# A fused attention and mixture-of-experts kernel: fewer float32 key tiles, a narrowing step through PSUM, two more early weight rooms, a new order of all steps

## The chip, the cores and the metric

The kernel runs on one core of one Trainium2 chip, in a single launch. The metric is the device time of that launch in microseconds (us). PE is the matrix engine, DVE the vector engine, ACT the scalar engine, POOL GpSimd; SP and ACT also issue DMAs. SBUF is the on-chip memory of 128 partitions, PSUM the accumulators that PE writes.

## The reference

Three stages follow each other. All inputs are float32, but `w_in` and `w_out` reach the kernel as float64.

```python
# attention: batch 2, heads 8, sequence 768, head size 64, 16 clusters
q_assign = np.argmax(np.einsum('bhsd,hcd->bhsc', q_n, c_n), axis=-1)   # k_assign alike
mask = q_assign[:, :, :, None] == k_assign[:, :, None, :]
scores = np.where(mask, scale * np.matmul(q, k.transpose(0, 1, 3, 2)), -1000000000.0)
scores = scores - np.max(scores, axis=-1, keepdims=True)
attn = np.exp(scores); attn = attn / (np.sum(attn, axis=-1, keepdims=True) + 1e-09)
x = np.matmul(attn, v)                       # then 1536 tokens x 512
# feed-forward with a gate, hidden size 2048
h = x @ w_in
g = h * np.clip(h + 3.0, 0.0, 6.0) / 6.0
x = (g @ w_out).astype(np.float32)
# soft mixture of 8 experts, 4 slots each, hidden size 1024
logits = x @ phi
d = softmax(logits, axis=0); slot_input = d.T @ x
slot_out[e] = np.maximum(slot_input[e] @ w1[e], 0.0) @ w2[e]
c = softmax(logits, axis=1); return c @ slot_out
```

(`softmax` stands here for the maximum, exponential and division that the reference writes out.)

## The kernel before

**Tiles.** The 16 pairs of batch and head are 16 heads, i = 0 to 15, each with 768 queries and 6 key tiles of 128 (t = 0 to 5). The 1536 tokens are 12 tiles of 128, called tokens 0 to 11 here; tokens 0 to 5 need heads 0 to 7, tokens 6 to 11 need heads 8 to 15. Values that need more than 16 bits are kept as a pair of float16 parts: `high` (an ACT copy to float16, L333) and `low` (POOL subtracts the high part, L343).

**A head.** PE computes masked scores for the row maxima (`sm`, L507), DVE reduces them (`mxs`, L523), PE computes scores again with the maxima folded in (`st`, L545 and L549), ACT takes the exponential, and `pv` multiplies the probabilities by the values. A key tile that `WHOLE` lists for its head goes through `pv` as float32: ACT writes `pp` once (L586) and PE does 6 float32 products (L615; the trace shows each as 2 matmuls, 12 for a tile). Any other key tile goes as a float16 pair: ACT writes `p` (L593) and its high part (L333), POOL the low part (L343), and PE does 6 + 6 + 6 float16 matmuls (L620, L621, L628). Score tiles stand in the PSUM pool `ps_s`, which has three rooms; `sm`, `st`, the transposes `gp` and others take turns in them.

**Weights of the feed-forward.** Half of each float64 word is handled at a time. `narrow` turns 1024 float64 a partition into float32: ACT takes the absolute value of the high word with a scale (L850), DVE shifts it left by 3 (L852), DVE joins the sign bit (L855), DVE joins the low word's top bits (L860). There are 16 of these, 8 of `wi` and 8 of `wod`, all in the time of heads 0 to 7. `wphi3` splits the product of `w_out` and `phi` into a high and a low part (L943, L945, L946).

**A token.** `hid` multiplies 128 tokens by the input weights (`h`, L684; a token is 48 matmuls of 512 columns), `act` forms the gate as a float16 pair `ghl`, and the pair is turned over, either by DMA transposes on SP's queue (L712) or, for tokens in `TURNED`, by PE (L721, to PSUM tiles `gp`) with two copies by ACT (L727) and two by DVE (L725). `gt` is one buffer for all tokens. `logits` (L736, L737) reads it.

**The tail.** Slot inputs (`zt`, `si`, `sit`), layer 1 of the experts (`e`, L1289), layer 2 (`o`, L1326 and, in column parts, L1346), then the slots' outputs are spread over the tokens (`so` L1241, `po` L1266) and written (L1279). Expert weights come in chunks of 1 MB named `wk_n`, two DMAs each on SP's queue (`fetch`, L1007; the last four in column parts, L988). Each chunk needs a room: `rooms` lists them in order. The first 4 are in ring a, 11 in ring b, 7 in buffers that the earlier stages free; the chunks after that wait until the first are used. `selectors` (L1230) is 24 small POOL copies that build a 0/1 matrix for `so`.

**What sets the order.** Every piece of work is a generator that is cut into steps at each `yield`; it is registered with `ev`, and the numbers in the string `ORDER` say from which generator the next step is taken. `ROOMS` fixes which buffer of its pool each tile takes. So the program order on each engine is written out, and each engine takes its instructions in that order; waits are by semaphores. A DMA queue's instruction waits for its buffer to be free, and what stands behind it on the same queue waits too.

## Time and profile before

| | us |
|---|---|
| three timed runs | 501.71, 502.46, 504.79 (median 502.46) |
| the profiled execution | 500.38 |
| its span in the trace | 498.2 |
| busy: PE, DVE | 447.5, 288.9 |
| busy: ACT, POOL | 314.1, 238.1 |

The span runs from the first instruction to the last; the profiled execution is 2.2 us longer than its span. Busy times are unions of the instructions' times on an engine; matmuls overlap each other there, so a busy PE is not PE at its peak. The page of the profile counts 93.4 MB by DMA.

### The profile page before, as it was taken

Reading aid. Unit: us, or ns where it says so; the run is one execution under the profiler, and the core shown is the slowest. Engines: PE = TensorE matmul, PEld = TensorE weight load, DVE = VectorE, ACT = ScalarE, POOL = GpSimd, SP = SyncE. Lnnn points to the kernel's source line nnn. Section 1 sums busy time; section 2 is a strip of 40 time slices with the busy share of each in tenths; the row PEclk is TensorE's granted clock in tenths of the full one; section 3 lists DMA queues with packets and bytes.
Section 4 is the critical chain, followed back from the end, with each engine's and each line's share of the span. In section 5 each row is a group of like instructions: output and inputs, shape, how many; then the busy total and the mean of one; then the engine's idle time right before and its main releaser. Section 6 shows DMA issues by size and latency. Waiting matters only on the chain.

```text
span 498.2 us, 11989 instructions
## 1 busy us (share of the span) xinstructions
PE 447.5 (90%) x5014; PEld 291.7 (59%) x5014; DVE 288.9 (58%) x489; ACT 314.1 (63%) x499; POOL 238.1 (48%) x217
## 2 busy tenths in 40 slices
PE   2699899998999989999999999979999999789773
PEld 1467787786876457556665766744555554623252
DVE  3889999898869665745728678412433254411322
ACT  4687888898865548778796977953445455501021
POOL 3435746856544336677686795973132236000000
PEclk9999999999999979999999999999999999889998
DMA  5799888659772985457559361018999305899996
GB/s 189 199 212 217 224 196 234 154 164 239 240 226 52 236 147 78 93 124 144 107 114 257 71 118 34 2 22 136 278 403 410 147 1 156 294 372 382 335 287 204
DMA packets 125622, 93.41 MB, mean 187 GB/s; under 512 B 88193, under 2 KB 111233, under 8 KB 125569
## 3 DMA queue, kind: packets, MB, share of 16 engines
q1 hardware_dynamic: 120832, 86.85, 65.7%
q10 hardware_dynamic: 4736, 5.80, 3.5%
q8 instruction: 39, 0.64, 0.5%
q14 instruction: 15, 0.11, 0.1%
HBM read 64.06 MB, written 7.34 MB: 143 GB/s over the span
## 4 chain that ended last, share of the span: by engine, by line
PE 53%; DVE 18%; DMA 8%; ACT 6%; POOL 6%; issue 6%; SPq 2%; DVEq 0%; POOLq 0%; ACTq 0%
PE h L684 15%; DVE mxs L523 5%; PE sm L507 5%; PE acc L615 5%; PE st L545 4%; PE st L549 4%; POOL ghl L343 3%; DMA wk<-in_moe_w_dram 3%; PE e L1289 2%; DMA wod<-in_moe_w_out_dram 2%; SPq L1007 2%; PE acc L628 2%; PE acc L620 2%; PE acc L621 2%; POOL pp L343 2%
## 5 line engine op out<-in xcount | busy, mean ns | idle before, releaser
L343 POOL TENSOR_TENSOR pp<-p,pp 128x768 f16<-128x768 f32 x62 | 105.4, 1707 | 71.0 <-ACT pp L333 26.4
L684 PE MATMUL h<-wq,xt 128*128 128x512 f16 x576 | 132.6, 379 | 0.6 <-DMA xt<-xhl 0.6
L523 DVE TENSOR_REDUCE mxs<-sm 128x1 f32<-128x768 f32 x96 | 88.7, 953 | 23.5 <-PE sm L507 22.9
L684 PEld LDWEIGHTS <-xt 128*128 128x128 f16 x576 | 55.2, 98 | 61.1 <-issue 1.3
L343 POOL TENSOR_TENSOR ghl<-r,ghl 128x1024 f16<-128x1024 f32 (+1 forms) x25 | 50.2, 2011 | 66.0 <-ACT ghl L333 65.9
L593 ACT ACTIVATE p<-st 128x768 f32<-128x768 f32 x62 | 49.9, 807 | 15.7 <-PE st L549 13.3
L333 ACT ACTIVATE pp<-p 128x768 f16<-128x768 f32 x62 | 52.0, 842 | 1.7 <-PE acc L628 0.5
L545 PE MATMUL st<-qk1t 128*128 128x384 f16 x192 | 48.7, 336 | 2.6 <-DVE qk2t L532 1.1
L615 PE MATMUL acc<-v,pp 128*128 128x65 f32 x408 | 50.1, 274 | 0.0
L615 PEld LDWEIGHTS acc<-v,pp 128*128 128x128 f32 x408 | 48.6, 192 | 1.7 <-ACT pp L586 0.3
L703 DVE SCALAR_TENSOR_TENSOR r<-r,h 128x1024 f32<-128x1024 f32 (+1 forms) x26 | 29.5, 1135 | 34.2 <-ACT r L701 34.2
L549 PE MATMUL st<-qk2t 102*128 102x384 f16 x192 | 48.6, 335 | 0.4 <-DVE qk2t L532 0.4
L507 PE MATMUL sm<-qk2t 80*128 80x384 f16 x192 | 45.6, 341 | 3.5 <-DVE qk2t L387 1.7
L343 POOL TENSOR_TENSOR qk<-qk,qk 128x768 f16<-128x768 f32 x15 | 26.8, 1787 | 30.3 <-ACT qk L333 29.7
L701 ACT ACTIVATE r<-h,b_relu 128x1024 f32<-128x1024 f32 (+1 forms) x26 | 27.2, 1047 | 19.0 <-POOL ghl L343 13.8
L333 ACT ACTIVATE ghl<-r 128x1024 f16<-128x1024 f32 (+1 forms) x26 | 25.7, 988 | 21.4 <-DVE r L703 19.7
L620 PE MATMUL acc<-v,pp 128*128 128x65 f16 x372 | 31.4, 193 | 2.0 <-DVE mv L494 1.9
L621 PE MATMUL acc<-v,pp 128*128 128x64 f16 x372 | 31.4, 194 | 0.0
L586 ACT ACTIVATE pp<-st 128x768 f32<-128x768 f32 x34 | 26.6, 808 | 6.9 <-PE st L549 6.7
L620 PEld LDWEIGHTS <-pp 128*128 128x128 f16 x372 | 27.0, 99 | 2.7 <-issue 0.3
L621 PEld LDWEIGHTS <-pp 128*128 128x128 f16 x372 | 25.4, 97 | 4.5 <-issue 2.4
L549 PEld LDWEIGHTS <-qk2t 102*128 102x128 f16 x192 | 19.2, 100 | 14.4 <-issue 2.5
(190 smaller groups left out, 792.3 us busy)
## 6 DMA issues: line engine op xcount, KB each, us to landing
wk<-in_moe_w_dram SPq DMA_DIRECT2D x60, 512.0 KB, 9.0
wi<-in_moe_w_in_dram SPq DMA_DIRECT2D x16, 512.0 KB, 5.6
wod<-in_moe_w_out_dram SPq DMA_DIRECT2D x16, 512.0 KB, 4.8
wos<-wo ACTq DMA_DIRECT2D x8, 512.0 KB, 4.5
wk<-wos SPq DMA_DIRECT2D x8, 512.0 KB, 5.9
qk<-in_q_dram SPq DMA_DIRECT2D x16, 192.0 KB, 3.3
qk<-in_k_dram SPq DMA_DIRECT2D x16, 192.0 KB, 3.7
v<-in_v_dram SPq DMA_DIRECT2D x16, 192.0 KB, 3.6
```

The costliest lines, as they stand in the source:

```text
L333: nc.scalar.activation(out, in_, AF.Copy, scale=scale)
L343: (nc.vector if e == "v" else nc.gpsimd).tensor_tensor(out=out, in0=in_, in1=hi, op=ALU.subtract)
L507: nc.tensor.matmul(s[:, j, 0:384], d["qk2t"][0:80, n, 0], d["qk2t"][0:80, 3 * j : 3 * j + 3, 1], start=True, stop=True,)
L523: nc.vector.tensor_reduce(out=mxs[i % 2][:, 96 + n : 97 + n], in_=s[:, :, 0:384], op=ALU.max, axis=AX.XY)
L545: nc.tensor.matmul(s[:, j, 0:384], d["qk1t"][:, t, 1], d["qk1t"][:, 3 * j : 3 * j + 3, 0], start=True, stop=False)
L549: nc.tensor.matmul(s[:, j, 0:384], d["qk2t"][0 : 96 + NT, t, 1], d["qk2t"][0 : 96 + NT, 3 * j : 3 * j + 3, 0], start=False, stop=True,)
L593: nc.scalar.activation(p32, s[:, :, 0:384], AF.Exp, scale=sc_exp)
L615: nc.tensor.matmul(o, p32[:, j, r * P : (r + 1) * P], d["v32"][:, t], start=(t == 0 and n == 0), stop=False)
L620: nc.tensor.matmul(o, hi, v1[:, t, 0:65], start=(t == 0 and n == 0), stop=False)
L621: nc.tensor.matmul(o[:, 0:64], hi, v1[:, t, 65:129], start=False, stop=False)
L684: nc.tensor.matmul(s[:, fb % 2], xt[:, lhs], wq[fb][:, hl, kk], start=(n == 0), stop=(n == 11))
L703: nc.vector.scalar_tensor_tensor(out=g, in0=r, scalar=6.0 * SG, in1=sf, op0=ALU.min, op1=ALU.mult)
```

## The change

1. `WHOLE` names three key tiles for each of heads 0 to 7 ("024") in place of 3 to 5: 24 float32 key tiles rather than 34.
2. `narrow`: DVE takes the sign bit first, from the high word into SBUF; ACT writes the absolute value to a PSUM tile `nt` of the pool `ps_s`; one DVE step shifts it and joins the sign, in place; the last DVE step joins the low word as before.
3. `wphi3`: ACT writes the high part from PSUM, one DVE step makes the low part from PSUM. The float32 copy `wpf` and one DVE copy are gone.
4. The first square root is called by a dummy (`warm_0`) right at the start of `centroids`, before the centroids are there.
5. `TURNED` loses tokens 8 and 9: their gates are turned by DMA.
6. `rooms` has two more entries: chunk 15 lies half in a buffer of the tokens' input tiles `xt` (now 3 buffers of two tokens) and half in the pool of the selector matrix; chunk 20 lies half in `xt` and half in a buffer of `r`. 24 chunks rather than 22 have a room before the first is used. Small tiles of the tail (`c16`, `cT`, `sel`, `s16`, `h1`, `hts`, `o2s`, `zts`, `sis`) lie in freed weight rooms.
7. `ORDER` and `ROOMS` are new from beginning to end; `selectors` stands after the slot inputs.

```diff
-    "2 2 2 1 3 9 3 9 10 10 2 2 10 10 10 10 10 11 280 1 8 6 11 12 32 12 325 96 178 280 292 84 84 137 137 80 80 284 36 "
+    "1 1 3 0 1 1 2 8 2 795 8 9 9 9 9 9 4 1 5 5 9 9 10 0 0 9 5 13 13 5 796 796 6 6 56 10 11 56 57 11 797 798 12 801 "
...
-WHOLE = ("01245", "01245", "01245", "0124", "024", "0124", "0124", "0124", "", "", "", "", "", "", "", "")
-TURNED = {6, 7, 8, 9, 10, 11}
+WHOLE = ("024", "024", "024", "024", "024", "024", "024", "024", "", "", "", "", "", "", "", "")
+TURNED = {6, 7, 10, 11}
...
     def centroids():
         c32 = ap.tile([P, D], F32, tag="acp", name="c32", bufs=1)
         nc.scalar.dma_start(out=c32, in_=cent.rearrange("h c d -> (h c) d"))
+        nc.gpsimd.memset(b_relu, 3.0 * SG)
+        nc.scalar.activation(sm.tile([P, 1], F32, tag="nm", name="warm_0", bufs=4), b_relu, AF.Sqrt)
...
         if part == 0:
-            t = ap.tile([P, 1024], U32, tag="nw", name=f"nw_{nm}", bufs=1)
-            raw[nm, "t"] = t
+            t = raw[nm, "t"] = pss(f"nt_{nm}").rearrange("p a b -> p (a b)").bitcast(U32)
+            s = raw[nm, "s"] = ap.tile([P, 1024], U32, tag="nw", name=f"nw_{nm}", bufs=1)
+            nc.vector.tensor_scalar(out=s, in0=hi, scalar1=0x80000000, scalar2=None, op0=ALU.bitwise_and)
+            yield
             nc.scalar.activation(t.bitcast(F32), hi.bitcast(F32), AF.Abs, scale=2.0**-111)
-            yield
-            nc.vector.tensor_scalar(out=t, in0=t, scalar1=3, scalar2=None, op0=ALU.logical_shift_left)
         elif part == 1:
             t = raw[nm, "t"]
             nc.vector.scalar_tensor_tensor(
-                out=t, in0=hi, scalar=0x80000000, in1=t, op0=ALU.bitwise_and, op1=ALU.bitwise_or
+                out=t, in0=t, scalar=3, in1=raw.pop((nm, "s")), op0=ALU.logical_shift_left, op1=ALU.bitwise_or
             )
...
-        wf = sm.tile([P, 4, NS], F32, tag="l4", name=f"wpf_{j}", bufs=1)
-        nc.scalar.activation(wf, po, AF.Copy, scale=SPH / SW)
-        yield
-        nc.vector.tensor_copy(wp2[:, 4 * j : 4 * j + 4, 0:NS], wf)
-        nc.vector.tensor_tensor(
-            out=wp2[:, 4 * j : 4 * j + 4, NS : 2 * NS], in0=wf, in1=wp2[:, 4 * j : 4 * j + 4, 0:NS], op=ALU.subtract
+        wh = wp2[:, 4 * j : 4 * j + 4, 0:NS]
+        nc.scalar.activation(wh, po, AF.Copy, scale=SPH / SW)
+        yield
+        nc.vector.scalar_tensor_tensor(
+            out=wp2[:, 4 * j : 4 * j + 4, NS : 2 * NS], in0=po, scalar=SPH / SW, in1=wh, op0=ALU.mult, op1=ALU.subtract
         )
...
-    rooms = ["a"] * NRA + ["b"] * NRB + ["w0", "w1", "w2", "w3", "ghl", "gt", "ghl"]
+    rooms = ["a"] * NRA + ["b"] * NRB + ["x.g", "w0", "w1", "w2", "w3", "x.r", "ghl", "gt", "ghl"]
+    rooms += ["a"] * 2 + ["b"] * 10
```

Three places show how the order moves work. The first is DVE at the start of head 0, before: `qk1t` and `qk2t` are the turned queries and keys, `as` and `mx` the cluster scores and their maxima, `nw_i0_0` and `wi_0_0` the first piece that is narrowed, `mxs` the row maxima.

```order
L387 COPY qk1t_0_152<-tq1_153 128x6x128
L436 TENSOR_REDUCE mx_0_212<-as_0_168 128x12
L437 TENSOR_TENSOR as_0_168<-as_0_168,mx_0_212 128x192
L445 TENSOR_TENSOR as_0_168<-as_0_168,rank_87 128x192
L448 TENSOR_REDUCE mx2_0_216<-as_0_168 128x12
L450 TENSOR_TENSOR oh_0_218<-as_0_168,mx2_0_216 128x6x2x16
L852 TENSOR_SCALAR nw_i0_0_247<-nw_i0_0_247 128x1024
L855 SCALAR_TENSOR_TENSOR nw_i0_0_247<-wi_0_0_222,nw_i0_0_247 128x1024
L860 SCALAR_TENSOR_TENSOR wi_0_0_222<-wi_0_0_222,nw_i0_0_247 128x1024
L387 COPY qk2t_0_257<-tq2_258 128x6x128
L523 TENSOR_REDUCE mxs_0_110<-sm_0_0_282 128x1
```

The same place after:

```order
L383 COPY qk1t_0_159<-tq1_160 128x6x128
L850 TENSOR_SCALAR nw_i0_0_240<-wi_0_0_153 128x1024
L432 TENSOR_REDUCE mx_0_248<-as_0_182 128x12
L433 TENSOR_TENSOR as_0_182<-as_0_182,mx_0_248 128x192
L441 TENSOR_TENSOR as_0_182<-as_0_182,rank_87 128x192
L444 TENSOR_REDUCE mx2_0_254<-as_0_182 128x12
L446 TENSOR_TENSOR oh_0_256<-as_0_182,mx2_0_254 128x6x2x16
L855 SCALAR_TENSOR_TENSOR nt_i0_0_239<-nt_i0_0_239,nw_i0_0_240 128x1024
L860 SCALAR_TENSOR_TENSOR wi_0_0_153<-wi_0_0_153,nt_i0_0_239 128x1024
L383 COPY qk2t_0_265<-tq2_266 128x6x128
L850 TENSOR_SCALAR nw_i0_1_314<-wi_0_1_262 128x1024
L519 TENSOR_REDUCE mxs_0_110<-sm_0_3_310 128x1
```

The sign step (L850) of a piece now stands ahead of the cluster maxima and does not need ACT; two steps rather than three stand between the one-hot matrix `oh` and the copy of `qk2t`, and the next piece's sign step stands ahead of the first row maximum.

The second place is SP's queue in the time of tokens 6 to 9, before: `xt_8` is the input of token 8, `wk_3` and the others are chunks of expert weights (`wos` is a product of `w_out` that the kernel wrote to memory itself).

```order
L669 DMA_TRANSPOSE xt_8_5502<-xhl_1_2904 128x8x128
L1007 DMA wk_3_5551<-wos_100 128x2x512 x2
L1007 DMA wk_4_5554<-in_moe2_w1_dram 128x1024
L1007 DMA wk_2_5470<-wos_100 128x2x512
L1007 DMA wk_4_5554<-in_moe2_w1_dram 128x1024
L1007 DMA wk_1_5468<-wos_100 128x2x512
L1007 DMA wk_5_6373<-in_moe2_w1_dram 128x1024
L1007 DMA wk_6_6375<-in_moe2_w1_dram 128x1024
```

After, `gt_8` and `gt_9` are the turned gates of tokens 8 and 9:

```order
L1011 DMA wk_12_6048<-in_moe2_w1_dram 128x1024
L1011 DMA wk_13_6050<-in_moe2_w1_dram 128x1024
L710 DMA_TRANSPOSE gt_8_6065<-ghl_8_5904 128x16x128 x2
L1011 DMA wk_4_5861<-in_moe2_w1_dram 128x1024
L1011 DMA wk_14_6105<-in_moe2_w1_dram 128x1024
L1011 DMA wk_1_5847<-wos_100 128x2x512
L1011 DMA wk_13_6050<-in_moe2_w1_dram 128x1024
L1011 DMA wk_0_4731<-wos_100 128x2x512
L1011 DMA wk_3_5852<-wos_100 128x2x512
L710 DMA_TRANSPOSE gt_9_6140<-ghl_9_6029 128x16x128
L1011 DMA wk_2_5849<-wos_100 128x2x512
L710 DMA_TRANSPOSE gt_9_6140<-ghl_9_6029 128x16x128
```

Four DMA transposes of gates now stand among the weight loads, where before only loads followed the last input transpose.

The third place is the end of SP's queue. Before, `wk_32` to `wk_35` are the last four chunks in column parts and `ob` the output tiles:

```order
L988 DMA wk_32_6721<-in_moe2_w2_dram 128x4x128
L988 DMA wk_33_6722<-in_moe2_w2_dram 128x4x128
L988 DMA wk_34_6723<-in_moe2_w2_dram 128x4x128
L1279 DMA out_0_dram<-ob_0_3_6912 128x2x256
L988 DMA wk_35_6724<-in_moe2_w2_dram 128x4x128
L1279 DMA out_0_dram<-ob_0_1_6901 128x2x256
```

After:

```order
L989 DMA wk_32_6959<-in_moe2_w2_dram 128x4x128
L989 DMA wk_33_6960<-in_moe2_w2_dram 128x4x128
L1296 DMA out_0_dram<-ob_0_3_6983 128x2x256
L989 DMA wk_34_6961<-in_moe2_w2_dram 128x4x128
L989 DMA wk_35_6962<-in_moe2_w2_dram 128x4x128
L1296 DMA out_0_dram<-ob_0_1_6993 128x2x256
```

Two weight loads rather than one stand behind the first output DMA.

## Rows read from the trace of the kernel before

**Rows 1.** Windows by stage: start and end, length, busy us of PE, PEld, DVE, ACT, POOL, PE clock.

```profile
25.00:331.00 306.00, 294.24 (x3534) 210.25 (x3533) 221.69 (x362) 240.76 (x366) 194.20 (x128) 0.99 0.65 150
...
336.00:425.00 89.00, 84.27 (x722) 45.60 (x722) 30.91 (x51) 43.72 (x75) 30.17 (x39) 1.00 0.69 221
425.00:450.00 25.00, 19.74 (x223) 10.09 (x224) 7.29 (x20) 5.07 (x16) 0.16 (x1) 0.86 0.91 336
```

**Rows 2.** Waits of PE: line, what it waited for, us in total, times, longest.

```profile
PE o L1346 <- DMA wk<-in_moe_w_dram: 3.3, 3, 2.4
```

**Rows 3.** Chain of waits, first 32 us: start, length, what.

```profile
3.53 1.28 ACT L815
4.82 0.21 ACT cy L815
```

**Rows 4.** Timeline of PE around a float32 and a float16 key tile: start, length, what.

```profile
36.53 1.45 PE L615 MATMUL acc<-v,pp 128*128 128x65 f32 x12
37.81 0.19 PE L620 MATMUL acc<-v,pp 128*128 128x65 f16 x1
...
38.18 1.25 PE L507 MATMUL sm<-qk2t 80*128 80x384 f16 x6
39.28 0.35 PE L628 MATMUL acc<-v,pp 128*128 128x65 f16 x6
39.46 1.75 PE L615 MATMUL acc<-v,pp 128*128 128x65 f32 x14
```

**Rows 5.** The page's groups: the float16 pairs' copies by POOL and ACT.

```profile
L343 POOL TENSOR_TENSOR pp<-p,pp 128x768 f16<-128x768 f32 x62 | 105.4, 1707 | 71.0 <-ACT pp L333 26.4
...
L333 ACT ACTIVATE pp<-p 128x768 f16<-128x768 f32 x62 | 52.0, 842 | 1.7 <-PE acc L628 0.5
```

**Rows 6.** Instructions by line: minimum, median, maximum in ns, first and last start.

```profile
L850 ACT ACTIVATE nw_i<-wi x8: 1131/1135/1143, 11.2 to 115.9; 128x1024 f32<-128x1024 f32 x8
L852 DVE TENSOR_SCALAR nw_o<-nw_o x8: 683/690/695, 86.4 to 185.6; 128x1024 uint32<-128x1024 uint32 x8
L855 DVE SCALAR_TENSOR_TENSOR nw_i<-wi,nw_i x8: 1224/1226/2295, 15.0 to 120.7; 128x1024 uint32<-128x1024 uint32 x8
L860 DVE SCALAR_TENSOR_TENSOR wo<-wod,nw_o x8: 1217/1226/2645, 96.7 to 188.3; 128x1024 uint32<-128x1024 uint32 x8
L945 DVE CAST wp<-wpf x4: 219/772/1672, 143.2 to 206.4; 128x128 f16<-128x128 f32 x4
L946 DVE TENSOR_TENSOR wp<-wpf,wp x4: 293/590/1629, 143.4 to 207.7; 128x128 f16<-128x128 f32 x4
L703 DVE SCALAR_TENSOR_TENSOR r<-r,h x26: 686/1213/1223, 176.9 to 424.5; 128x1024 f32<-128x1024 f32 x22, 128x512 f32<-128x512 f32 x4
```

**Rows 7.** Timeline of POOL and DVE at one narrowing step.

```profile
112.75 1.65 POOL L343 TENSOR_TENSOR pp<-p,pp 128x768 f16<-128x768 f32 x1 [2.25 <-ACT pp L333]
112.84 2.65 DVE L860 SCALAR_TENSOR_TENSOR wo<-wod,nw_o 128x1024 uint32<-128x1024 uint32 x1
```

**Rows 8.** Chain of waits, 380 to 414 us.

```profile
397.84 0.89 PE gp L721 x16
398.73 5.18 PE h L684 x24
```

**Rows 9.** Landing of the 12 gate transposes that SP issues at L712.

```profile
DMA to landing us min/median/max: 4.2/4.9/7.6
```

**Rows 10.** DMA in 336 to 430 us: GB/s in 40 slices of 2.35 us.

```profile
GB/s 64 167 47 211 192 169 321 241 209 363 288 405 409 413 415 408 411 406 413 410 404 415 394 105 0 3 0 7 0 0 0 0 0 94 199 258 211 352 396 77
```

**Rows 11.** Chain of waits, 425 us to the end.

```profile
465.07 8.90 DMA wk<-in_moe_w_dram
...
480.02 4.76 DMA out_dram<-ob
...
484.79 4.05 DMA wk<-in_moe_w_dram
```

**Rows 12.** Timeline of POOL around the selectors.

```profile
415.81 3.66 POOL L1230 COPY sel<-ident 32x4 f32<-32x4 f32 x24
```

More of the change, by code (lines that the diff above doesn't have):

```diff
@@ L289, in clustered_attention_ffn_softmoe @@
     mvs = [ap.tile([P, 129], F16, name=f"mv_{i}", bufs=1) for i in range(3)]
-    def first():
-        nc.gpsimd.memset(b_relu, 3.0 * SG)
-        yield
-        nc.scalar.activation(sm.tile([P, 1], F32, tag="nm", name="warm_0", bufs=4), b_relu, AF.Sqrt)
     def second():
@@ L961, in clustered_attention_ffn_softmoe, with room @@
     rings = {"a": ring_a}
-    def room(n):
-        m = rooms[n % len(rooms)]
+    def room(n, m, size, nm):
         if m in rings:
-            return rings[m].tile([P, 2048], F32, tag="w", name=f"wk_{n}")
+            return rings[m].tile([P, size], F32, tag="w", name=nm)
+        if m == "g":
+            return rings["cw"].tile([P, size], F32, tag="g", name=nm)
         if m[0] == "w":
-            return wi.tile([P, 2048], F32, tag=m, name=f"wk_{n}")
-        return mo.tile([P, 2048], F32, tag=m, name=f"wk_{n}", bufs=2 if m == "ghl" else 1)
+            return wi.tile([P, size], F32, tag=m, name=nm)
+        return mo.tile([P, size], F32, tag=m, name=nm, bufs={"ghl": 2, "xt": NT // 2}.get(m, 1))
     def fetch():
@@ L978, in fetch @@
             for j in range(4):
-                ts.append(room(n + j).rearrange("p (c d) -> p c d", c=8))
-                wt_[kind, e + j, hf] = ts[j]
+                ts.append(room(n + j, rooms[n + j], 2048, f"wk_{n + j}").rearrange("p (c d) -> p c d", c=8))
+                wt_[kind, e + j, hf] = (ts[j][:, 0:4], ts[j][:, 4:8])
             for c0, w in PARTS:
@@ L1020, in phs_load @@
         yield
-    ev(first)
     ev(consts)
@@ L1108, in clustered_attention_ffn_softmoe, with lt2k @@
         evf()
-    for n in range(7):
+    for n in range(9):
         evf()
-    def xt2k(shape, dt, nm):
+    late = {}
+    def lt2k(k, a, shape, dt):
+        if k not in late:
+            if k[0] == "w":
+                t = wi.tile([P, 2048], F32, tag=k, name=f"late_{k}")
+            elif k == "x":
+                t = mo.tile([P, 1024], F32, tag="xt", name="late_x", bufs=NT // 2)
+            else:
+                t = rings[k[0]].tile([P, 2048], F32, tag="w", name=f"late_{k}")
+            late[k] = t
         n = 1
-        for x in shape[1:]:
+        for x in shape:
             n *= x
-        t = mo.tile([P, 2048 // mybir.dt.size(dt)], dt, tag="xt", name=nm, bufs=NT)[:, 0:n]
-        if len(shape) == 3:
-            t = t.rearrange("p (a b) -> p a b", a=shape[1])
+        t = late[k].bitcast(dt)[:, a * 2048 // mybir.dt.size(dt) : a * 2048 // mybir.dt.size(dt) + n]
+        if len(shape) == 2:
+            t = t.rearrange("p (a b) -> p a b", a=shape[0])
+        elif len(shape) == 3:
+            t = t.rearrange("p (a b c) -> p a b c", a=shape[0], b=shape[1])
         return t
@@ L1128, in zsum @@
         last = mt[NTOK - 1]
-        adiag = rings["cw"].tile([P, P], F32, name="adiag")
+        adiag = nident
         nc.vector.tensor_scalar(out=adiag, in0=ident, scalar1=last["al"], scalar2=None, op0=ALU.mult)
@@ L1200, in combine_weights @@
         yield
[L1201 to L1203 removed]
+        sl["c16"] = lt2k("a0", 0, [NTOK, 4, NS], F16)
         c16 = sl["c16"]
@@ L1217, in combine_weights @@
         yield
-        cT = sl["cT"] = rings["cw"].tile([P, NTOK, P], F16, name="cT")
+        cT = sl["cT"] = lt2k("a0", 2, [NTOK, P], F16)
         nc.vector.tensor_copy(cT[:, 0:NT], tp[:, 0:NT])
@@ L1222, in selectors @@
     def selectors():
-        sel = sl["sel"] = rings["cw"].tile([P, NG, 3, NS], F32, name="sel")
+        sel = sl["sel"] = lt2k("a1", 0, [NG, 3, NS], F32)
         nc.gpsimd.memset(sel, 0.0)
@@ L1268, in combine @@
         if p == len(PARTS) - 1:
-            ob = xt2k([P, 512], F32, f"ob_{p}_{u}")
+            ob = rings["b"].tile([P, 2048], F32, tag="w", name=f"ob_{p}_{u}")
         else:
@@ L1298, in relu @@
     def relu(g):
-        h1 = sl["h1", g] = mo.tile([P, 8, P], F32, tag="r", name=f"h1_{g}")
+        h1 = sl["h1", g] = lt2k("b0", 2 * g, [8, P], F32)
         for f in range(2):
```

56 lines of the change are left out of this document (31 added, 25 removed), and 319 rows, old and new, of tables (ORDER, ROOMS).

## The prediction

> **What bounds the kernel now.** I read the windows by stage first, then the chain of waits in the stages that the change touches, then the durations of the lines that it edits. In attention, 25 to 331 us, PE is busy for 294.2 of 306 us and no other engine for more than 241 [rows 1]: time taken from PE there is nearly all worth having, time put on ACT or POOL has room, and 11.8 us is the most that better waiting could give. In tokens 6 to 11, 336 to 425 us, PE is busy 84.3 of 89 [rows 1], so PE decides again. In the tail DMA does: PE waits 3.3 us for weights in the last layer [rows 2], a weight load of 8.90 us stands on the chain at 465, and at the end an output DMA of 4.76 us is followed by a last weight load of 4.05 [rows 11]. The loads are late because they had no room: DMA runs near 410 GB/s, then at 0 to 7 GB/s for nine slices, and begins again when the input weights' rooms are freed [rows 10].
>
> **The start.** Before, the first square root's table load, 1.28 us, stands on the chain behind the centroids' arrival [rows 3]. The dummy now loads it while ACT waits for that DMA; the exponential's table goes in early too, and I count it at nothing, since ACT waits for the turned queries there. Ahead of the copy of `qk2t` DVE now has two narrowing steps rather than three; the third, 0.69 [rows 6], moves ahead of the cluster maxima, where it may still delay them, so I count 0.2 of it. Term: −1.5, between 0 (if the first queries are what comes late) and −2.0 (both in full).
>
> The trace shows the square root 0.01 us behind the end of its table load [rows 3]. The Trainium skill (ScalarE: Activation LUTs, "What ACT_TABLE_LOAD costs") gives about 1.28 us for the load and 1.38 more for a drain at each switch. By that the term would be −2.9 and the forecast 489.1; no drain is visible behind this load, so the sum stays with the row.
>
> **Ten key tiles, float32 to float16 pairs.** A float32 tile holds PE from 36.53 to 37.81, 1.28 us. A pair takes 37.81 to 38.18, 0.37 us, and the low parts 39.28 to 39.46, 0.18 us: 0.55 [rows 4]. Ten tiles save 10 x 0.73 = 7.3 us of PE. They add 10 x 0.84 = 8.4 us to ACT's 240.8 and 10 x 1.71 = 17.1 us to POOL's 194.2 [rows 1, 5]; both stay under 250 of 306, and what hides them is PE's work on other tiles of the same head. With that cover gone PE would wait up to 0.84 + 1.71 = 2.55 us for a tile, 25 us for ten; with it, nothing.
>
> **Narrowing, 16 times.** Before, DVE needs 0.69 + 1.23 + 1.23 = 3.15 us for each [rows 6]. After: the shift with the sign reads PSUM, and the nearest row with an operand in PSUM, L703, has 1.21; the last step stays at 1.23. The new sign step has no row: it is at least 0.69, the one-input step from SBUF to SBUF (L852), and at most 1.23, a full-rate step (L855), because its source is every second word. I take 0.69, since it has one input and both ends in SBUF as L852 has. So DVE's work is 0 to 16 x 0.54 = 8.6 us more, and I take 0. ACT's 1.14 stays. The middle value now holds one of three score rooms for at least 1.14 + 1.21 + 1.23 = 3.6 us, 16 times. What stands behind it: `sm`, `st` and the transposes that want a room, and with them PE. Three to two rooms costs between 0 and 3.6 us each, never less than 0. I take 0 here and give the other end to a rival.
>
> **Splitting the gate's weights.** The two DVE steps of `wphi3` take 0.22 to 1.67 and 0.29 to 1.63; from minimum, median and maximum of four their sum is 3.4 + 3.1 = 6.5 us [rows 6]. One step from PSUM replaces them, near the lower 0.29, so about 1.2: DVE −5.3.
>
> **DVE beside POOL.** One step of L860 took 2.65 us where its fellows take 1.23; it started 0.09 us after a POOL subtraction of 1.65 us and ended 1.09 after that one's end, close to one undisturbed step: it waited and then ran [rows 7]. L855 has one such (2.30), and the long ones of L945 and L946 look the same [rows 6]. Such waiting comes to 1.42 + 1.07 + (6.5 − 4 x 0.51) = 7.0 us in all.
>
> The Trainium skill (SBUF — State Buffer, "Who interferes with whom") states that a DVE instruction with two SBUF inputs, or in a two-port mode, shuts out a GpSimd instruction that reads SBUF, and the reverse; with at most one SBUF input and outside these modes it doesn't. Rows 7 agrees. By that the two joining steps and the new split leave the conflict, since each has one input in PSUM now, while the sign step, if it runs at 0.69, may still meet it.
>
> **Attention's term.** PE's 7.3 would be the term if PE decided everywhere. It has 11.8 us of waits in the stage, and where another engine or a weight transfer ends last, a shorter `pv` only becomes a longer wait. I take three quarters, −5.5. Bounds: −9.8 (all 7.3, and 2.5 from narrowing steps that no longer meet POOL) and, without the rivals, 0.
>
> **Tokens 8 and 9.** PE loses 64 transposes of 0.89/16 = 0.056 us: −3.6 [rows 8]. ACT and DVE lose copies that lie off the path. The four DMA transposes must land before `logits`. In attention they landed in 4.9 us, at most 7.6 [rows 9]; the cover is the hidden matmuls of the next token, about 36 of them ahead of `logits`, 36 x 5.18/24 = 7.8 us [rows 8]. A pair one after the other needs 9.8 to 15.2 us, so 0 (both under way together) to 7.4 us is left open a token, 0 to 14.8 for both, nearer to 0 because the first half is sent while the second is still formed. But here they queue on SP among weight loads at 410 GB/s [rows 10], which no row shows. I take 1 us each. Weight loads that SP holds back behind a transpose cost nothing: DMA idles some 21 us afterwards [rows 10]. Term: −1.6, between −3.6 and +11.
>
> **Selectors.** 3.66 us of POOL stood ahead of token 11's low parts [rows 12]; now they follow the slot inputs, beside DMA-bound layers. 0 to −3.7; token 11 had other PE work meanwhile, so I take −0.5.
>
> **The tail.** Two more chunks, 2.1 MB, are loaded in the idle stretch; at 410 GB/s that is 5.1 us that the late loads save [rows 10]. PE can use only what it waits for: 3.3 us [rows 2] and a little in layer 2, so −3.5. Against it, two of the last loads stand behind the first output DMA instead of one. The last load was issued when that DMA had landed [rows 11], so I expect both to be, and one more load of 0.26 MB at 336 GB/s [rows 1] is +0.8. Term: −2.7, between −5.1 and +0.8.
>
> **Sum.** −1.5 − 5.5 − 1.6 − 0.5 − 2.7 = −11.8 against the profiled execution's 500.38, which is 488.6. The median of the runs is 2.1 above that execution, so on its scale 490.6; I say 490.5. Below, all times are on that scale.
>
> **Rivals.**
> *A, slower: the lost PSUM room.* Each `nt` holds a room while PE, with three, is busy 96% of the stage. If PE then waits p us at each of 16 narrowings, the gain is gone at p = 0.74 and the kernel is over 1% slower from 1.06; at p = 1.1 it takes 490.5 + 17.6 = 508. For it: with three rooms PE seldom waits today, and nothing shows that two would do. Against it: narrowings come one at a time, and an `nt` is held only while DVE works on it, when row maxima would wait for DVE anyway. 0.14.
> *B, gate transposes late.* If both tokens leave 5 us open instead of 1, 498.5. For it: the load on DMA; against it: 7.8 us of cover. 0.12.
> *C, the sign step at full rate, and DVE decides in heads 0 to 7.* 8.6 us more on DVE, of which I'd count 6.5 on the path, as it eats attention's gain: 497. For it: the source's stride. 0.13.
> *D, POOL and DVE free of each other.* The rule above, in this kernel: the 7.0 us of DVE waiting go and also come back to PE, of which 4 us beyond my sum: 486.5. For it: rows 7; against it: DVE isn't the engine that decides over the whole stage. 0.10.
> *E, the change doesn't do what it says:* what the new order gains in one place it loses in another, and only the start and half of the tail remain: 500. 0.07.
>
> **How the numbers follow.** The forecast has 0.44, and 484 to 497 as its own range, which is the sum with each term some way to its bounds. 481 to 503 leaves out A (0.14) and the tails of the forecast and D. No change means within 1% (497.4 to 507.5), about what a measurement of this kernel can tell. Faster by more: the forecast nearly whole (0.42), D (0.10), half of C (0.07), a third of B (0.04), together 0.63; slower by more: A and a little of B, 0.15; between them 0.22.
>
> **What the profile after would show.** Start: the table load ahead of the centroids' arrival. Attention: L615's successor 288 matmuls, PE's busy time in the stage near 287, and its end 6 to 8 us earlier; a wait of PE for DVE's last narrowing step at score lines would be A. The sign step's duration, 0.69 or 1.2, settles C; narrowing steps never above 1.3 would be D. Tokens: `logits` waiting for DMA is B. Tail: no wait of PE for weights in the last layer, and two loads landing after the first output DMA. The forecast is wrong if attention's end moves by less than 3 us or the tail, from token 11's end, is as long as before.

## The result, and the profile after

The changed kernel takes 488.95 us (median of 4 runs, 484.83 to 490.43) against 503.6 for the kernel before (4 runs, 501.71 to 504.79): a ratio of 0.970, interval 0.964 to 0.976. The profiled execution of the changed kernel took 484.83, the fastest of its runs, with a span of 483.1; a second one (`a_again`, below) has a span of 484.5, is the fastest of its own four runs too, and is used beside it. Where some of a run's executions are over 1.5% slower than its fastest at a lower granted clock, they are left out of the median given below.

The windows by stage of the changed kernel answer to [rows 1]; the columns are the same, and the last row is the tail, from the first `zt` step to the end.

```profile
25.00:319.00 294.00, 283.38 (x3583) 202.23 (x3584) 214.84 (x351) 242.43 (x369) 201.31 (x134) 1.00 0.64 147
324.00:409.00 85.00, 80.69 (x658) 41.90 (x657) 28.44 (x47) 40.57 (x70) 27.30 (x15) 1.00 0.92 269
417.00:483.00 66.00, 51.45 (x557) 25.70 (x557) 15.63 (x34) 8.30 (x18) 4.52 (x26) 0.84 0.91 295
```

Attention ends 12 us earlier, with 10.9 us less of PE's busy time in it and about as much idle time, 10.6 us, as before. Of the 10.9, some 3 us are the clock (an estimate, explained below): before, PE ran at half clock for 6.8 us of this stage, here for none of it. What is left is about the ten tiles' 7.3. Tokens 6 to 11 are 4 us shorter. The tail is not: 66.0 us, 65.7 before.

The instructions by line (minimum, median, maximum in ns) answer to [rows 6]: sign step, shift with sign, last step, and the one split step.

```profile
L850 DVE TENSOR_SCALAR nw_i<-wi x8: 682/694/695, 10.3 to 114.8; 128x1024 uint32<-128x1024 uint32 x8
L850 DVE TENSOR_SCALAR nw_o<-wod x8: 683/712/2068, 96.1 to 173.1; 128x1024 uint32<-128x1024 uint32 x8
...
L855 DVE SCALAR_TENSOR_TENSOR nt_o<-nt_o,nw_o x8: 1232/1233/1233, 96.9 to 179.1; 128x1024 uint32<-128x1024 uint32 x8
...
L860 DVE SCALAR_TENSOR_TENSOR wo<-wod,nt_o x8: 1220/1220/1222, 98.8 to 180.4; 128x1024 uint32<-128x1024 uint32 x8
...
L945 DVE SCALAR_TENSOR_TENSOR wp<-wpo,wp x4: 283/292/292, 130.1 to 196.6; 128x128 f16<-128x128 f32 x4
```

No step with an operand in PSUM takes longer than 1.233 us, though 27 of the 36 overlap work of POOL; before, with both operands in SBUF, single ones took up to 2.65. The sign step runs at 0.69 us, with its strided source, and it alone still has long ones, up to 2.07; the three longest each began less than 1 us behind the start of a POOL subtraction.

The page's group of the pairs' copies by POOL answers to [rows 5]; the mean is 1.65 us now, 1.71 before:

```profile
L339 POOL TENSOR_TENSOR pp<-p,pp 128x768 f16<-128x768 f32 x72 | 118.5, 1651 | 52.9 <-ACT pp L329 23.9
```

PE's waits (what for, us in total, times, longest) answer to [rows 2], and the landing of the gate transposes to [rows 9].

```profile
PE acc L624 <- POOL pp L339: 2.0, 2, 1.2
...
PE o L1363 <- DMA wk<-in_moe_w_dram: 1.7, 3, 0.9
...
PE lg L734 <- DMA gt<-ghl: 0.4, 1, 0.4
```

```profile
DMA to landing us min/median/max: 4.3/4.7/7.7
```

PE's waits for POOL's low parts have not grown with the ten new pairs: 2.0 us, 2.4 before. `logits` waits 0.4 us for a transposed gate. No row of PE's waits names a narrowing step.

DMA's GB/s in 40 slices of 1.25 us, from 380 to 430 us, answer to [rows 10]; the idle stretch is gone:

```profile
GB/s 418 262 388 346 82 166 282 271 256 249 210 256 275 354 416 419 419 419 419 423 393 410 393 419 406 406 419 403 410 393 400 380 406 321 341 331 360 397 410 419
```

How far along heads 5 and 7 are in several profiles is read from PE's timeline at their last matmul (start, length). First the kernel before:

```profile
125.23 0.19 PE L636 MATMUL acc<-mv,qk2t 128*128 128x64 f16 x1
...
154.68 0.19 PE L636 MATMUL acc<-mv,qk2t 128*128 128x64 f16 x1
```

The changed kernel, first profile:

```profile
120.28 0.19 PE L632 MATMUL acc<-mv,qk2t 128*128 128x64 f16 x1
...
149.92 0.19 PE L632 MATMUL acc<-mv,qk2t 128*128 128x64 f16 x1
```

The changed kernel again (`a_again`):

```profile
119.34 0.19 PE L632 MATMUL acc<-mv,qk2t 128*128 128x64 f16 x1
...
152.78 0.19 PE L632 MATMUL acc<-mv,qk2t 128*128 128x64 f16 x1
```

Head 5 ends 5 to 6 us earlier than before in both, head 7 by 4.8 in one and 1.9 in the other. The rest of attention's gain comes after head 7.

Profiles can only be compared together with PE's granted clock. It stands at 1.00 (2.4 GHz) for most of the span and at 0.50 (1.2 GHz) in single stretches. One such stretch of `a_again`, the wait of PE that ended just before it, and the 12 products of one float32 key tile in this stretch and behind it:

```profile
138.97 0.37 PE L541 MATMUL st<-qk1t 128*128 128x384 f16 x1 [2.85 <-ACT p L589]
```

```profile
139.10:145.90 6.80, 6.80 (x51) 5.07 (x50) 5.59 (x5) 3.94 (x5) 1.64 (x1) 0.50 0.57 125
```

```profile
140.29 2.46 PE acc L611 x12
...
147.53 1.29 PE acc L611 x12
```

The same products take 1.9 times as long, so about half of the time that PE is busy in such a stretch is lost to it (an estimate from these two rows). The stretches fall differently in every profile, even of one program:

| profile | head 5's end to head 7's, us | of it at half clock | head 7's end to attention's end | of it at half clock |
|---|---|---|---|---|
| before | 29.5 | 0 | 175.9 | 6.8 |
| `b_gate`, the same program up to token 8 | 32.4 | 10.2 | 174.8 | 3.4 |
| changed kernel, first profile | 29.6 | 0 | 169.0 | 0 |
| `a_again`, the same program | 33.4 | 6.8 | 169.7 | 3.4 |
| `a_sp`, the same but for the tail | 37.8 | 20.5 | 169.2 | 0 |
| `a_34` | 30.1 | 0 | 168.7 | 3.4 |
| `a_old_dve` | 34.1 | 3.4 | 174.9 | 3.4 |

### The profile page after: what moved, and what is told of

It is laid out like the page before. It is cut to its first block, busy times and chain, and to the rows that moved or that the text cites. A ratio compares the mean times of both kernels' runs of the same rounds, so it can differ in the third digit from the quotient of the medians.

```text
span 483.1 us, 12003 instructions
## 1 busy us (share of the span) xinstructions
PE 436.5 (90%) x5010; PEld 282.1 (58%) x5010; DVE 281.7 (58%) x481; ACT 314.8 (65%) x502; POOL 249.7 (52%) x227
## 4 chain that ended last, share of the span: by engine, by line
PE 56%; DVE 15%; DMA 13%; ACT 5%; POOL 3%; issue 3%; SPq 3%; ACTq 0%; DVEq 0%; POOLq 0%
PE h L682 21%; DVE mxs L519 6%; PE st L541 4%; PE st L545 3%; PE sm L503 3%; PE acc L611 3%; PE e L1306 3%; DMA qk1t<-qk 3%; DMA out_dram<-ob 2%; DMA wod<-in_moe_w_out_dram 2%; PE acc L616 2%; PE acc L617 2%; DMA xt<-xhl 2%; DMA wi<-in_moe_w_in_dram 2%; PE acc L624 2%
## 5 line engine op out<-in xcount | busy, mean ns | idle before, releaser
L339 POOL TENSOR_TENSOR pp<-p,pp 128x768 f16<-128x768 f32 x72 | 118.5, 1651 | 52.9 <-ACT pp L329 23.9
L589 ACT ACTIVATE p<-st 128x768 f32<-128x768 f32 x72 | 57.8, 805 | 11.8 <-PE st L545 9.7
L329 ACT ACTIVATE pp<-p 128x768 f16<-128x768 f32 x72 | 60.0, 840 | 1.6
L701 DVE SCALAR_TENSOR_TENSOR r<-r,h 128x1024 f32<-128x1024 f32 (+1 forms) x26 | 29.5, 1136 | 38.1 <-ACT r L699 37.8
L616 PE MATMUL acc<-v,pp 128*128 128x65 f16 x432 | 36.2, 192 | 0.3 <-DVE mv L490 0.2
L617 PE MATMUL acc<-v,pp 128*128 128x64 f16 x432 | 36.1, 194 | 0.0
L611 PEld LDWEIGHTS acc<-v,pp 128*128 128x128 f32 x288 | 34.7, 192 | 1.4 <-ACT pp L582 0.3
L339 POOL TENSOR_TENSOR qk<-qk,qk 128x768 f16<-128x768 f32 x15 | 24.7, 1647 | 20.9 <-ACT qk L329 20.0
L611 PE MATMUL acc<-v,pp 128*128 128x65 f32 x288 | 35.5, 273 | 0.0
L616 PEld LDWEIGHTS <-pp 128*128 128x128 f16 x432 | 31.2, 99 | 4.6 <-issue 0.8
L617 PEld LDWEIGHTS <-pp 128*128 128x128 f16 x432 | 29.2, 96 | 2.6
L329 ACT ACTIVATE qk<-qk 128x768 f32<-128x768 f32 (+2 forms) x32 | 26.1, 816 | 5.6 <-DMA qk1t<-qk 3.4
```

The costliest lines, as they stand in the source:

```text
L329: nc.scalar.activation(out, in_, AF.Copy, scale=scale)
L339: (nc.vector if e == "v" else nc.gpsimd).tensor_tensor(out=out, in0=in_, in1=hi, op=ALU.subtract)
L589: nc.scalar.activation(p32, s[:, :, 0:384], AF.Exp, scale=sc_exp)
L611: nc.tensor.matmul(o, p32[:, j, r * P : (r + 1) * P], d["v32"][:, t], start=(t == 0 and n == 0), stop=False)
L616: nc.tensor.matmul(o, hi, v1[:, t, 0:65], start=(t == 0 and n == 0), stop=False)
L617: nc.tensor.matmul(o[:, 0:64], hi, v1[:, t, 65:129], start=False, stop=False)
```

## The experiments

Twelve runs in three groups; each group ran on one chip, and "before" beside it had medians of 500.1, 500.7 and 501.1 us. Times are medians of 4 runs, or of as many as are named, with their extremes. The control, `a_again`, is of the second group, so a distance of 1 us from it says little for runs of the other two.

**a_34: 34 float32 tiles again.**

```diff
-WHOLE = ("024", "024", "024", "024", "024", "024", "024", "024", "", "", "", "", "", "", "", "")
+WHOLE = ("01245", "01245", "01245", "0124", "024", "0124", "0124", "0124", "", "", "", "", "", "", "", "")
```

> The changed kernel with the 34 float32 key tiles of before (all else, the order too, as changed). In the changed kernel's profile the last accumulation of attention starts at 318.9 us, in the kernel before at 330.6. Theory PE (PE's saved time is the gain): ten tiles cost 7.3 us of PE again, attention ends 5.5 to 7.3 us later, and the whole takes about 495 rather than 489. Theory DVE (the narrowing freed of POOL is the gain): at most 2 us later. Theory order (the new order is the gain): at most 3 us later.

490.07 us (489.24 to 492.78), 1.1 more than the control's 489.01. The timeline of PE, as above:

```profile
126.75 0.19 PE L632 MATMUL acc<-mv,qk2t 128*128 128x64 f16 x1
...
156.82 0.19 PE L632 MATMUL acc<-mv,qk2t 128*128 128x64 f16 x1
```

Eight of the ten tiles are done by head 5's end; PE's sum for them is 8 x 0.73 = 5.8 us, and they cost 6.5 there against the changed kernel's first profile and 7.4 against the control (126.75 against 120.28 and 119.34). At head 7's end it is 6.9 against the first profile, where neither has a stretch at half clock in between; against the control only 4.0 seem left, but the control had 6.8 us at half clock there. Attention's end is 6.6 and 3.0 us later, with 3.4 us at half clock in attention against 0 and 10.2; with half of these differences allowed for (an estimate) that is 4.9 and 6.4. At the end of the span 4.4 and 3.0 are left, in the medians 1.1, with a higher mean clock in `a_34`'s runs (0.975 to 0.978 against 0.955 to 0.975). So theory PE fits attention. Its "about 495" for the whole was not seen; what the tiles are worth there, the runs leave open between 1 and 4.4 us.

**a_old_dve: the narrowing and splitting of before.**

```diff
-            t = raw[nm, "t"] = pss(f"nt_{nm}").rearrange("p a b -> p (a b)").bitcast(U32)
-            s = raw[nm, "s"] = ap.tile([P, 1024], U32, tag="nw", name=f"nw_{nm}", bufs=1)
-            nc.vector.tensor_scalar(out=s, in0=hi, scalar1=0x80000000, scalar2=None, op0=ALU.bitwise_and)
+            t = raw[nm, "t"] = ap.tile([P, 1024], U32, tag="nw", name=f"nw_{nm}", bufs=1)
             yield
             nc.scalar.activation(t.bitcast(F32), hi.bitcast(F32), AF.Abs, scale=2.0**-111)
...
+            nc.vector.tensor_scalar(out=t, in0=t, scalar1=3, scalar2=None, op0=ALU.logical_shift_left)
             nc.vector.scalar_tensor_tensor(
-                out=t, in0=t, scalar=3, in1=raw.pop((nm, "s")), op0=ALU.logical_shift_left, op1=ALU.bitwise_or
+                out=t, in0=hi, scalar=0x80000000, in1=t, op0=ALU.bitwise_and, op1=ALU.bitwise_or
```

> The changed kernel with the narrowing and the splitting of before (middle value in SBUF, three steps with two SBUF inputs in two of them, no room of the score pool held); the first step's place in the order is left empty and the shift stands ahead of the sign step. Theory PE: attention's end moves by under 1.5 us, although some narrowing steps take 2.3 to 2.7 us again. Theory DVE: 4 to 7 us later, about the 7.0 us of waiting that the kernel before has. Rival A (the lost PSUM room costs): earlier, and the whole faster than 489.

518.0 us (512.07 to 519.08, three runs): 29.0 more than the control, far outside every theory's number. The instructions by line, as above, and then POOL and DVE at one narrowing, from the timeline:

```profile
L853 DVE TENSOR_SCALAR nw_i<-nw_i x8: 683/864/1884, 12.3 to 139.9; 128x1024 uint32<-128x1024 uint32 x8
...
L854 DVE SCALAR_TENSOR_TENSOR nw_i<-wi,nw_i x8: 1224/1824/3049, 13.0 to 141.4; 128x1024 uint32<-128x1024 uint32 x8
...
L859 DVE SCALAR_TENSOR_TENSOR wi<-wi,nw_i x8: 1225/1954/3023, 15.6 to 143.7; 128x1024 uint32<-128x1024 uint32 x8
```

```profile
69.28 1.88 DVE L853 TENSOR_SCALAR nw_i<-nw_i 128x1024 uint32<-128x1024 uint32 x1
70.57 5.65 POOL L339 TENSOR_TENSOR wq<-wi,wq 128x1024 f16<-128x1024 f32 x2
71.19 3.05 DVE L854 SCALAR_TENSOR_TENSOR nw_i<-wi,nw_i 128x1024 uint32<-128x1024 uint32 x1
74.28 3.02 DVE L859 SCALAR_TENSOR_TENSOR wi<-wi,nw_i 128x1024 uint32<-128x1024 uint32 x1
```

Three steps that need 3.15 us undisturbed take 7.95 beside POOL's subtractions, which are stretched too (5.65 for two; one takes 2.11 to 3.10 in this run). DVE's groups of the narrowing add up to 73.1 us here, to 53.2 in the changed kernel; with the split steps DVE is busy 309.6 us rather than 281.7. 73.1 − 16 x 3.15 = 22.7 us of it are more than the steps need undisturbed. PE then waits for these steps, here for the last narrowing step of a piece and for the second split step:

```profile
215.69 0.44 PE L919 MATMUL tp<-ident,wo 128*128 128x128 f32 x2 [1.98 <-DVE wo L859]
...
232.49 0.19 PE L734 MATMUL lg<-wp,gt 128*128 128x64 f16 x1 [2.02 <-DVE wp L946]
```

From 15 us to attention's end, first the control and then this run (start and end, length, PE's busy time, and the clock as the eighth number):

```profile
15.00:322.70 307.70, 292.01 (x3630) 207.08 (x3630) 223.91 (x364) 249.67 (x380) 207.93 (x142) 0.98 0.63 147
```

```profile
15.00:354.83 339.83, 305.20 (x3630) 216.21 (x3630) 250.91 (x370) 251.06 (x380) 221.25 (x142) 0.94 0.58 134
```

The stage is 32.1 us longer: PE idles 34.6 us rather than 15.7, and its 3630 matmuls, as many in both, take 13.2 us more at a lower clock. So DVE's lost time isn't the kernel's loss one for one: 18.9 us of this stage's loss are waits of PE, the rest is the clock. What the kernel before lost in narrowing and splitting, 7.0 us of DVE's time, was so little because its order kept DVE and POOL apart more; the new order doesn't. (One `nw` buffer is also held across more steps here than in the order's plan, which adds some serial waiting; its share was not separated.)

**a_34_old_dve: both undone,** by both edits above.

> Both of these undone together, the new order kept. If the two parts are the whole gain in attention, its last accumulation starts at 329 to 331 us again, as before. If the order carries a part, it starts earlier than 327; if the parts add up, the delay is the sum of the two single ones.

530.6 us (527.28 and 533.93, two runs), with attention's last accumulation ending at 361.9 us against 330.8 before. Neither 329 to 331 nor 327 or less was met: the new order, on its own with the old steps, is 30 us slower than the old kernel beside it. Against the changed kernel's first profile attention ends 42.8 us later, about the sum of the two single delays, 6.6 and 35.7, as the last expectation had it; in the medians the parts don't add up (1.1 + 29.0 is not 41.6). The clock has a large part in these sums: here PE is at half clock for 54.6 us before attention's end, 41 of them at a stretch, and beside `a_34` its matmuls are busy for 27.0 us more and it idles 9.1 us more. What brought on the long stretch stays open.

**a_no_warm: without the dummy square root.**

```diff
-        nc.scalar.activation(sm.tile([P, 1], F32, tag="nm", name="warm_0", bufs=4), b_relu, AF.Sqrt)
```

> The changed kernel without the dummy square root, so that the table is loaded when the centroids have come. The prediction's term: 1.3 us later at the first row maxima (PE's first sm at 17.8 rather than 16.5 us) and about 1.3 us on the whole. If the first narrowing or the queries' transposes end last there, under 0.4 us.

490.71 us (489.08 to 493.2), 1.7 more than the control, within its spread. PE's first `sm` starts at 18.8 us, 2.9 later than the control's 15.9 and 2.3 later than the first profile's 16.5, so more than the table load was saved there. Nothing of it is lost on the way to head 5, which ends at 122.8 us, 3.2 and 2.3 later than in these two.

**a_again, a_ob, a_sp, a_tail: the tail.** `a_again` is the changed kernel itself. `a_ob` moves two output tiles to other rooms:

```diff
-            ob = (ring_a if p else rings["b"]).tile([P, 2048], F32, tag="w", name=f"ob_{p}_{u}")
+            ob = (ring_a if p and u % 2 == 0 else rings["b"]).tile([P, 2048], F32, tag="w", name=f"ob_{p}_{u}")
```

with `ob_1_1:3` and `ob_1_3:4` in `ROOMS` (2 and 3 before). `a_sp` moves one number of `ORDER`, so that the first output DMA of SP stands behind the last two weight loads; `a_tail` does both.

> The changed kernel itself, as the control of the three beside it: about 489 us, PE's first zt step to the end of the span 65.8 us, as in its first profile (65.7 in the kernel before).

> The changed kernel with the output tiles ob_1_1 and ob_1_3 in two other rooms of ring b, so that they don't share the rooms of ob_1_0 and ob_1_2, whose output DMAs are under way. Theory rooms: DVE's wait of 1.28 us for the output DMA at 474.2 goes, the last column part starts that much earlier, and the tail takes about 64.5 rather than 65.8 us. Rival (the last weight loads decide anyway): under 0.3 us.

> The changed kernel with the first output DMA of SP's queue behind the last two weight loads rather than ahead of them. Theory queue (the prediction's +0.8 for two loads behind an output DMA): the loads go out at about 462 rather than 465.5 us and the tail gains 0.8 to 3 us. Rival: the output DMA is late instead and its landing ends last, gain under 0.5 us.

> Both of these. If they are two separate waits on the path, their gains add up, 2 to 4 us, and the tail takes 62 to 64 us; if the one hides the other, no more than the larger of the two.

| | median us (extremes) | tail in the profile, us |
|---|---|---|
| a_again | 489.01 (486.19 to 492.83) | 64.8 |
| a_ob | 486.93 (484.87 to 489.47) | 63.3 |
| a_sp | 489.09 (487.61 to 490.14) | 64.7 |
| a_tail | 487.24 (485.72 to 490.24) | 63.1 |

The timeline of the changed kernel shows SP's queue and then DVE at the place that `a_ob` and `a_sp` change:

```profile
465.05 0.38 SPq L1296 DMA_DIRECT2D out_dram<-ob  x1
465.48 1.07 SPq L989 DMA_DIRECT2D wk<-in_moe_w_dram  x2
```

```profile
474.24 1.18 DVE L1291 TENSOR_SCALAR ob<-po 128x384 f32<-128x384 f32 x2 [1.28 <-DMA out_dram<-ob]
475.44 0.29 DVE L1269 SCALAR_TENSOR_TENSOR late_a<-so,late_a 32x128 f16<-32x128 f32 x1
```

In `a_ob` DVE's row at this place has no wait:

```profile
477.64 1.02 DVE L1291 TENSOR_SCALAR ob<-po 128x384 f32<-128x384 f32 x2
```

DVE waited 1.28 us for an output DMA, because the new `ROOMS` puts `ob_1_1` where `ob_1_0` is still being written out, and behind DVE's copy stood the next part's last step (L1269). With other rooms the tail is 1.5 us shorter, about as expected. The tail's length alone would not show it: in eight profiles with the changed kernel's tail it lies between 63.9 and 66.2 us, with 10.7 to 21.9 us of it at half clock. The part behind layer 2's last matmul does: 8.6 and 8.7 us in `a_ob` and `a_tail`, 10.0 to 10.5 in those eight and in `a_sp`. The two loads behind the output DMA cost nothing that can be seen (64.7 against 64.8). `a_ob` has the lowest median; its distance from the control, 2.1 us, is within the spread of the runs.

**a_nowod and a_34_nowod: without the last four loads of output weights.** Blocks 2 and 3 of `w_out` are not loaded, and their narrowing reads a constant; so these two compute something else from there on.

```diff
     def wout_load(j, hf):
+        if j >= 2:
+            raw["o", j, hf] = None
+            yield
+            return
```

> The changed kernel without the last four loads of the output weights (blocks 2 and 3; their narrowing reads a constant instead, so the output is not the reference's). Control, the changed kernel again: head 5 ends at 119.5 us, head 7 at 153.0, first hidden matmul 160.1. Theory wait (the transfers and narrowings of these blocks, not PE, set the end of heads 6 and 7): head 7 ends 3 to 8 us earlier. Theory PE: within 1 us of 153.

> The same loads left out, with the 34 float32 key tiles of before. With the loads, 34 tiles end head 5 at 126.9 us (7.4 later than 24 tiles) but head 7 at 157.0 (150 to 157). Theory wait: without the loads the distance stays, head 7 ends 5 to 8 us later than in the run beside it, and so does the whole. Theory PE absorbed elsewhere: under 3 us.

483.7 us (481.32 and 486.16, two runs) and 491.35 (490.19 to 493.58). Head 7's last matmul in the two:

```profile
149.99 0.19 PE L632 MATMUL acc<-mv,qk2t 128*128 128x64 f16 x1
```

```profile
157.76 0.19 PE L632 MATMUL acc<-mv,qk2t 128*128 128x64 f16 x1
```

Without the loads the ten tiles cost 7.8 us at head 7's end, with 3.4 us at half clock up to there in both profiles, and 5.1 in the spans. With the loads it was 6.9 and 4.4 against the first profile, with no half clock up to there in either; the 4.0 and 3.0 against the control are in part its clock. The chain of waits of the control has the load between heads 5 and 7, and PE's wait of 2.85 us stands behind it:

```profile
129.61 7.38 DMA wod<-in_moe_w_out_dram
```

So the load does make PE wait, but theory wait's 3 to 8 us are not there: the changed kernel's first profile, with its loads, ends head 7 at 149.92, and without them it is 149.99, with 3.4 us at half clock. The loads take up about 1 us of what the ten tiles save.

**b_24: the kernel before with 24 float32 tiles.** `WHOLE` as in the change, in `ORDER` the low part of each new pair right behind its high part, and a buffer of its own for the new float32 values.

> The kernel before with 24 float32 key tiles and nothing else, the low parts of the ten new pairs in the order right behind their high parts, their float32 values in one more buffer. PE's 7.3 us are saved at head 5's end (125.4 before) if PE decides there: 118 to 121. If POOL's extra 17 us meet DVE's narrowing in the old order: 123 to 130. The whole: theory PE 494 to 497, theory wait 499 to 502, more meetings of POOL and DVE over 502.

529.55 us (524.07 to 531.03), 28 more than before; head 5 ends at 147.3 us, outside all that was expected. POOL's wait for the high parts, from the waits of before and of this run:

```profile
POOL pp L343 <- ACT pp L333: 26.4, 16, 5.8
```

```profile
POOL pp L249 <- ACT pp L239: 61.4, 26, 9.8
```

POOL takes its instructions in order, and with the low parts put in at once it stands and waits 35 us more, while what is behind it waits too. From 15 us to attention's end, before and in this run:

```profile
15.00:330.80 315.80, 301.81 (x3600) 215.37 (x3598) 229.88 (x370) 248.48 (x377) 199.82 (x134) 0.99 0.66 151
```

```profile
15.00:360.96 345.96, 317.51 (x3660) 225.63 (x3659) 237.38 (x370) 256.81 (x387) 222.24 (x144) 0.92 0.59 138
```

PE idles 14.5 us more and is busy 15.7 us more, although it has the ten tiles less: over half of this stage's loss is the clock. So the tiles are no gain by themselves; they need an order made for them. (It was this placement of the low parts that was tried, no better one.)

**b_gate: the kernel before with tokens 8 and 9 turned by DMA.**

```diff
-TURNED = {6, 7, 8, 9, 10, 11}
+TURNED = {6, 7, 10, 11}
```

> The kernel before with the gates of tokens 8 and 9 turned by DMA and nothing else. From the last accumulation's end to the first zt step 101.7 us before, 97.0 to 98.0 in the changed kernel. The prediction's term: 1.6 us shorter, 3.6 at most. Rival B: up to 6 us longer, with PE waiting for the transposes ahead of logits.

510.53 us (508.09 to 513.0), 9.4 more than before. From the last accumulation's end to the first `zt` step it takes 99.5 us, 2.2 less than before. But the tail takes 75.8, 10.1 more. (In this profile attention, the same program as before, also ends 5.2 us later, at half clock for 20.5 us rather than 6.8; that is not the change's.) The timeline of SP's queue, and PE's waits, show why the tail is late:

```profile
383.99 24.63 SPq L712 DMA_TRANSPOSE gt<-ghl  x4
408.66 20.60 SPq L1007 DMA_DIRECT2D wk<-in_moe_w_dram  x20
```

```profile
PE o L1326 <- DMA wk<-in_moe_w_dram: 9.1, 3, 6.2
```

Here the four transposes stand ahead of nearly all weight loads, and while they wait for the gates, SP issues none of them. The order of the change spreads them:

```profile
366.00 7.55 SPq L710 DMA_TRANSPOSE gt<-ghl  x2
373.59 1.73 SPq L1011 DMA_DIRECT2D wk<-in_moe_w_dram  x2
...
381.04 5.42 SPq L710 DMA_TRANSPOSE gt<-ghl  x1
...
387.19 3.52 SPq L710 DMA_TRANSPOSE gt<-ghl  x1
```

## Why the prediction was right, point by point

The time, 490.5, is 1.5 us above the measured 488.95, and the change is faster as forecast. That the sum came so near is in part luck: it counted on 2.7 us in the tail, which gave 0 to 0.9, and on 2.1 in the tokens and selectors, which gave 3.7 to 4.7, and these two errors cancel. The gain itself was forecast at 12.0 us and came out at 14.7 here and at 11.7 in the group of `a_again`. By one of its own signs, "the tail, from token 11's end, is as long as before", the forecast would even have been wrong in the first profile: from token 11's last `logits` matmul to the end it takes 70.0 us there and 67.9 in `a_again`, 68.3 before.

- *The start, −1.5.* PE's first `sm` starts 1.5 us earlier in one profile and 2.1 in the other, and undoing the dummy costs 2.3 to 2.9 us there and as much at head 5. But head 0 then ends 2 to 3 us later than before (46.6 and 45.6 us against 43.3): what was won at the first maxima, the new order spends again in head 0.
- *Ten key tiles, −7.3 of PE.* The time is there: 6.5 to 7.4 us at head 5's end for the eight tiles until then, more than PE's 5.8, and 6.9 at head 7's end between two profiles without a stretch at half clock. "I take three quarters", −5.5, is about what `a_34` shows at attention's end (4.9 to 6.4 with the clock allowed for). The reason that was given for the missing quarter, transfers that end last, is not shown: leaving out the loads behind head 5 changes the tiles' worth by about 1 us.
- *Narrowing, 0.* The sign step's 0.69, the 1.23 of the others and no wait of PE for the PSUM room were right, so C and A fell. But the prediction priced the freedom from POOL at the 7.0 us of DVE that the kernel before lost, and counted none of it but a bound of 2.5. In the new order that freedom is worth up to 29.0 us (`a_old_dve`), part of it by the clock: the old order had kept POOL's and DVE's work more apart. D's mechanism, that DVE's freedom comes back to PE, is there behind head 7 (next point), though its 486.5 was too low by 2.5. The rule of the Trainium skill that was weighed (SBUF — State Buffer, "Who interferes with whom") says that a DVE step contends with a GpSimd instruction that reads SBUF if it has two SBUF inputs or runs in a two-port mode, and not if it has at most one and runs in none. The trace agrees: no step with one operand in PSUM was longer than 1.233 us beside POOL, while the one-input sign step at its fast rate took up to 2.07.
- *Attention as a whole, −5.5 after the start's −1.5.* The last accumulation ends 11.7 us earlier in the first profile and 8.1 in `a_again`, 1 to 5 more than the −7.0 of both. Some 3 us of the 11.7 are the clock: the profile before had 6.8 us at half clock in attention, the first profile after none. Six to seven us of both numbers arise after head 7, where the sum had no term. The first part of this document places all narrowing in the time of heads 0 to 7; in the trace of before, two of the 16 pieces and three of the four splits come after head 7. At one split, DVE's two steps, stretched beside POOL's subtractions (169.65 to 173.20 us), hold up the steps of a head, PE waits twice, and the 6.8 us at half clock follow from 176.5 on:

```profile
170.02 1.67 DVE L945 CAST wp<-wpf 128x128 f16<-128x128 f32 x1
171.72 1.63 DVE L946 TENSOR_TENSOR wp<-wpf,wp 128x128 f16<-128x128 f32 x1
...
175.40 0.19 PE L620 MATMUL acc<-v,pp 128*128 128x65 f16 x1 [1.94 <-DVE mv L494]
...
177.05 0.80 PE L507 MATMUL sm<-qk2t 80*128 80x384 f16 x2 [1.11 <-DVE mxs L523]
```

  After the change no wait of PE above 1.3 us is left between head 7 and attention's end. With the old steps put back into the new order (`a_old_dve`) the stretch from head 7 to attention's end takes 174.9 us, as in the old order (174.8 in `b_gate`, with as much at half clock), against 169.0 to 169.7 in the changed kernel. So this part of the gain comes with the new steps; the new order alone does not have it.
- *Tokens 8 and 9, −1.6, and the selectors, −0.5.* From attention's end to the first `zt` step 101.7 us became 98.0 and 97.0, so −3.7 and −4.7. The gates alone are −2.2 (`b_gate`), and `logits` waits 0.4 us, so B fell. The sentence that SP's held-back loads cost nothing is wrong as it stands: in the old order they cost 10 us in the tail. In the new one no such cost is seen: the loads are spread, and DMA has no idle stretch left to hide them in.
- *The tail, −2.7.* It gained −0.9 in `a_again` and nothing in the first profile, which has 21.6 us at half clock in the tail against 17.7 and, before, 11.1. The part that was expected came: PE's waits for weights in layer 2 fell from 4.7 us to 1.0 to 1.7, and layer 2's last matmul ends 2.0 us (first profile) and 3.2 us (`a_again`) sooner after `zt` than before. +0.8 for the queue was wrong (`a_sp`: nothing), and some 1.5 us are lost in a wait that the prediction didn't see, for output rooms (`a_ob`).

E, that the gains are lost again elsewhere and the whole takes 500, falls with the measured time. `a_34_old_dve` and `b_24` show that the parts need each other: the new order without the new steps and with the old tiles is 41.6 us slower than the changed kernel, and the fewer tiles without the new order are 28 slower than the old one, in both cases with over 50 us at half clock before attention's end. No run has the new steps in the old order.
